# A list-ordered kernel for attention and a squared-ReLU MLP: SyncE's issues counted in the order, and other due times

## The chip, the cores and the metric

The kernel runs on one core of one Trainium2 chip. The core has five engines that each work through their own instructions in order: TensorE (PE in the profile; its weight loads are shown as PEld), VectorE (DVE), ScalarE (ACT), GpSimd (POOL) and SyncE (SP), which here issues all the DMA transfers. The metric is the time of one execution on the device in microseconds (us); less is better.

## The reference, cut to what matters

Four batches of 12480 rows of 128 numbers pass through two attention steps with 32 inducing rows, and then through an MLP with a squared ReLU:

```python
def mab(q, kv):
    s = scale * (q @ kv.transpose(0, 2, 1))
    s = s - s.max(-1, keepdims=True)
    a = np.exp(s)
    a /= a.sum(-1, keepdims=True) + 1e-09
    return a @ kv
h = mab(I, x)        # 32 x 128 for each batch: needs all 12480 rows
out = mab(x, h)      # 12480 x 128
...
r = np.maximum(out @ w_in, 0.0)      # d_ff = 2048
return (r * r) @ w_out
```

So each batch has a first softmax over all of its rows, which gives h, and only then a second softmax for each row, and the MLP.

## The kernel before, in words

**The work.** Each batch is cut into 26 chunks of 480 rows (104 chunks in all), and the chunks into 7 groups of four (the last group has two). As the second attention step is linear in h, the kernel multiplies h with the weights first and writes the squared ReLU as sums over pairs of the 32 attention weights. What is left for each chunk is, by the names of the jobs in the code:

- `ups` (L1035): four matmuls from the attention weights `dT` into `hp`, two at a time;
- `lifts` (L1051): two ScalarE squares of `hp` into `g`;
- `downs` (L1063): five matmuls into `po`, the last of which (L1075) takes `dT` with `lin`;
- `evictions` (L1082): `po` to `o`, on ScalarE or VectorE; `stores` (L1096): one DMA to the output.

Around the chunks lie, for each batch:

- `x_loads` (L588): 7 loads of x transposed into 7 buffers `xp`; `row_loads` (L597): 13 loads of half a group of x rows into 5 buffers `xnb`, the last of them made of 5 DMAs;
- `first_softmax` (L607): scores of a group against the inducing rows (8 fp32 matmul instructions, L369 with `indT_sb`), evicted by VectorE with a running maximum (L625); then the maximum over all; then `exponents` (L655, ScalarE), `transposes` (L663, VectorE, L671), and `row_sums` (L676), where TensorE multiplies the exponents with the rows (L694), which ends in h (L715);
- `readings` (L719): scores of a group against h (L369 with `hT`), which is the last use of that group's `xp` buffer; then `attention` (L745), nine steps over VectorE, GpSimd and ScalarE that end with a DMA of the weights to a scratch tensor `ad` (L781);
- `squares` (L785): three DMAs that load `dT` back (L516), and then `square` (L798): a small matmul `sq` (L805), a VectorE eviction (L813), a GpSimd square (L819), and one DMA for each chunk of the group that puts the result into the last 32 rows of `dT` (L822). The group's `downs` need it;
- `prepare` (L826), `pair_weights` (L994) and `pair_sums` (L1013): from h to the batch's weights.

The first softmax of batch 0 runs ahead of all that, in a function of its own.

**The order.** From there to the end, the order of the instructions on each engine is written out when the program is built. Each job above is a generator that yields operations. `op(engines, took, due, *needs)` names the engine, a cost in us, a due time and marks or rings of buffers that must be free. The class `Order` (L77) keeps a clock for each engine. At each step it finds the operation that could start earliest; among the operations of that engine that could start within PATIENCE of it, it takes the one with the earliest due time (L120 to L123). So a due time is a rank among those that are ready, and not a time at which anything starts. Once the program runs, an engine takes its instructions in the order found, and waits for what isn't there.

The due times hang on three things. `nominal(n)` is LEAD + PERIOD x n for chunk n; a batch's first chunk is n = 26 b. `h_due(b)`, the due time of h, is that of the chunk AHEAD chunks before the batch's first (L585). A group's X, around which attention and squares are placed, is a fixed time ahead of its first chunk, with SLACK in it (L726, L790). The numbers before are PERIOD 2.95, LEAD 33.0, SLACK 6.0, AHEAD 17.

**SyncE in the order.** An operation on SP costs SyncE 0.06 us, however many DMAs it has. `moved` is the time at which the transfers so far have been moved. No SP operation starts before `moved - QUEUED`, with QUEUED 3.0:

```python
if engines == "SP":
    return max(t, self.free["SP"], self.moved - QUEUED), "SP"
...
    self.free["SP"] = start + 0.06
    self.moved = max(self.moved, start) + took
    end = max(start + LAND, self.moved + LAND - 0.7)
```

Of the kernel before, what the change touches and what calls it, by code (L numbers as in the profile page):

```python
# [25 lines left out]
CH = 4 * TP  # L26
# [16 lines left out]
SLOTS = 8  # L43
PERIOD = 2.95
LEAD = 33.0
SLACK = 6.0
AHEAD = 17
QUEUED = 3.0
PATIENCE = 0.12
SPARE = 0.3  # L50
LAND = 3.2
LATE = {"PE": 0.25, "ACT": 0.2, "DVE": 0.15, "POOL": 0.25}
# [24 lines left out]
class Order:  # L77

    def __init__(self):
        self.free = {"PE": 0.0, "ACT": 0.0, "DVE": 0.0, "POOL": 0.0, "SP": 0.0}  # L80
        self.moved = 0.0
        self.jobs = []

# [13 lines left out]
    def when(self, job):  # L97
        engines, took, due, needs, alone = job[1]
        t = 0.0 if alone else job[2]
        for n in needs:  # L100
            r = n.ready()
            if r is None:
                return None
            t = max(t, r)
        if engines == "SP":
            return max(t, self.free["SP"], self.moved - QUEUED), "SP"
        if "|" in engines:
            act, dve = max(t, self.free["ACT"]), max(t, self.free["DVE"])
            return (act, "ACT") if act + SPARE < dve else (dve, "DVE")
        return max(t, self.free[engines]), engines  # L110

    def run(self):
        while self.jobs:
# [11 lines left out]
            if engine == "SP":  # L125
                self.free["SP"] = start + 0.06
                self.moved = max(self.moved, start) + took
                end = max(start + LAND, self.moved + LAND - 0.7)
            else:
                self.free[engine] = start + took  # L130
                end = start + took + LATE[engine]
# [4 lines left out]

def op(engines, took, due, *needs, alone=False):
    return engines, took, due, needs, alone


@with_exitstack
def attend_then_relu2_mlp(ctx: ExitStack, tc: tile.TileContext, xn, xT, indT, w_in, w_out, outT):
# [445 lines left out]
    def x_loads():  # L588

        for b in range(1, NB):  # L590
            for G, w in enumerate(WID):
                end = yield op("SP", 2.6 * w / CH, h_due(b) - 30 - 2.0 * (NG - G), xp_ring, alone=True)
                xp_ring.held.append(mark("read", b, G))
                sts[b].xp[G] = load_xT(b, G, flow, NX)
                mark("x", b, G).t = end

    def row_loads():  # L597

        for b in range(1, NB):
            for h in range(HALVES):  # L600
                i = h % XB
                end = yield op("SP", 1.4, h_due(b) - 24 + 1.3 * h, xnb_free[i], alone=True)
                sts[b].rows[h] = load_half(b, h, xnb[i])
# [3 lines left out]
    def first_softmax():  # L607

        for b in range(1, NB):
# [5 lines left out]
            for G, w in enumerate(WID):  # L615
                due = H - 23 - 1.2 * (NG - G)
                yield op("PE", 0.85, due, att, mark("x", b, G))
# [37 lines left out]
    def exponents(b, sT, nb, zs):  # L655

        for G, w in enumerate(WID):
            end = yield op("ACT", 0.69, h_due(b) - 17 + 2.0 * G, mark("nb", b), alone=True)
            s = sT[:, 480 * G:480 * G + w]
# [3 lines left out]
    def transposes(b, sT):  # L663

        sts[b].en = {}
        for G, nb32 in enumerate(BLK):
            end = yield op("DVE", 0.62, h_due(b) - 15.5 + 2.0 * G, mark("exp", b, G), en_ring, alone=True)
            mark("summed", b, G)
# [7 lines left out]
    def row_sums(b, zs):  # L676
# [5 lines left out]
        for G, nb32 in enumerate(BLK):  # L682
            for h in range(2 * G, min(2 * G + 2, HALVES)):
                needs = [mark("rows", b, h), mark("en", b, G)] + ([] if hacc else [att])
                t0 = 8 * (h - 2 * G)
                t1 = min(t0 + 8, nb32)
                end = yield op("PE", 0.075 * (t1 - t0), H - 14 + 2.0 * G, *needs)
                if hacc is None:
# [30 lines left out]
    def readings():  # L719

        for b in range(NB):
            st = sts[b]
            for G in range(NG):
                w, t = WID[G], BLK[G]
                wb = 32 * t
                X = nominal(NCH * b + 4 * G) - 14 - SLACK  # L726
                due = X - 9
                if b < NB - 1:
                    due = min(due, h_due(b + 1) - 32 - 2.0 * (NG - G))
                end = yield op("PE", 0.85, due, att, mark("h", b))  # L730
# [14 lines left out]
    def attention(b, G, e, X, since, gone):  # L745
# [33 lines left out]
        nc.vector.scalar_tensor_tensor(a16[:, 1, 0:w], a[:, 0:w], lessen, a16[:, 0, 0:w], op0=ALU.add, op1=ALU.subtract)  # L779
        end = yield op("SP", 0.7, X)  # L780
        nc.sync.dma_start(st.ad[:, :, :, 480 * G:480 * G + w].rearrange("q i h n -> (q i) h n"), a16[:, :, 0:w])  # L781
# [3 lines left out]
    def squares():  # L785

        for b in range(NB):
            st = sts[b]
            for G, n in enumerate(GRP):
                X = nominal(NCH * b + 4 * G) - 11 - SLACK  # L790
                rows = slice(0, MI * n)
                end = yield op("SP", 1.1, X, mark("ad", b, G), dT_ring, alone=True)
                dT_ring.held.append(mark("over", b, G))
# [4 lines left out]
    def square(b, G, n, X, rows, dT):  # L798

        st = sts[b]  # L800
        yield op("PE", 0.1 * n, X + 4, mark("dT", b, G), mark("single", b), po_ring)
        done = po_ring.take()
        ps = ps_o.tile([P, 512], F32, tag="po", name=f"sq_{b}_{G}")
        for j in range(n):
# [3 lines left out]
            )  # L808
        end = yield op("DVE", 0.72, X + 4.2, z_ring)
        done.t = end  # L810
        done = z_ring.take()
        z = mlp.tile([P, CH], F32, tag="z", name=f"z_{b}_{G}", bufs=2)
        nc.vector.tensor_scalar(z[rows], ps[rows, 0:CH], st.off[rows], cut[rows], op0=ALU.add, op1=ALU.max)  # L813
        end = yield op("POOL", 1.05, X + 5.5, zz_ring)
        done.t = end
# [3 lines left out]
        nc.gpsimd.tensor_tensor(g[rows], zv[rows], zv[rows], op=ALU.mult)  # L819
        end = yield op("SP", 0.12 * n, X + 7)  # L820
        for j in range(n):
# [274 lines left out]
    def stores():  # L1096

        for n, (b, c) in enumerate(CHUNKS):
            end = yield op("SP", 0.65, nominal(n + 1.5), mark("out", n), alone=True)
            nc.sync.dma_start(outT[:, b, c], outs.pop(n))  # L1100
            mark("stored", n).t = end
# [216 lines left out]
```

## Time and profile before

| what | value |
|---|---|
| runs | 429.43, 425.01, 428.63 us; median 428.63 |
| the profiled execution | 426.38 us |
| its span, from the first to the last instruction | 424.6 us |
| mean granted TensorE clock | 0.958 |
| instructions | 8741 |
| moved by DMA | 94.29 MB, 222 GB/s |

How to read the profile: it is one execution, with times in us unless marked ns. A row of a group names the line, the engine, the operation, what is written and read (`out<-in`), the shapes and the count; then come the busy time, the mean duration in ns, the idle time of the engine just before these instructions, and what ended most of it. In a row of one line of the source, the three durations are least, median and greatest in ns. In a table of stretches each row is a stretch in us from the start of the span, with each engine's busy time in it, the granted TensorE clock as a share of full speed (PEclk), and the share of the DMA engines. SPq is SyncE's queue of DMA issues; a row `A <- B` of a table of waits says that A waited for B, in us in total, times, and longest.

### The profile page before, as it was taken

The page shows a single profiled execution, that of the slowest core. Times are in us where ns is not written, and L with a number is a line of the kernel's source. Part 1 is how long each engine was busy: PE and PEld are TensorE (multiplying, and loading weights), DVE is VectorE, ACT ScalarE, POOL GpSimd, SP SyncE. Part 2 cuts the span into 40 slices and gives each one's busy share as a digit, 9 for nine tenths or more (in the row PEclk, how much of TensorE's full clock was granted, in tenths as well). Part 3 has the DMA queues.
Part 4 walks back from the last instruction along what each step waited for, and adds up shares of the span by engine and source line. Part 5 has one row for each costly group of instructions (what it writes and reads, how often), then busy time and mean ns, then how long its engine had stood idle before and what let it go on. Part 6 is the DMA issues. An engine that isn't in the chain of part 4 may idle for free.

```text
span 424.6 us, 8741 instructions
## 1 busy us (share of the span) xinstructions
PE 357.0 (84%) x3077; PEld 169.2 (40%) x3077; DVE 329.9 (78%) x879; ACT 285.4 (67%) x394; POOL 83.3 (20%) x93
## 2 busy tenths in 40 slices
PE   0993736999789799989889899998799999998894
PEld 0662504533334245423434254324344455333341
DVE  7859889899566499989844789989646999997541
ACT  1464231477967498666966795769676987886894
POOL 1000011151210122242300312142110302343010
PEclk9997985799899899999999999999899999999999
DMA  7972566645596998856797978954985243456742
GB/s 273 416 248 64 188 248 223 209 150 170 144 334 211 329 345 259 294 173 214 209 354 234 322 271 264 325 182 152 293 289 168 95 154 106 159 153 212 209 142 96
DMA packets 63760, 94.29 MB, mean 222 GB/s; under 512 B 22880, under 2 KB 53856, under 8 KB 63712
## 3 DMA queue, kind: packets, MB, share of 16 engines
q1 hardware_dynamic: 63712, 93.69, 66.9%
q8 instruction: 25, 0.41, 0.4%
q14 instruction: 23, 0.19, 0.1%
HBM read 58.52 MB, written 31.95 MB: 213 GB/s over the span
## 4 chain that ended last, share of the span: by engine, by line
PE 46%; DVE 25%; DMA 16%; ACT 6%; issue 4%; SPq 2%; DVEq 0%; ACTq 0%
PE po L1074 12%; PE hp L1045 11%; DMA xnb<-xn_dram 7%; PE s L369 7%; DMA dT<-ad 4%; DMA ad<-a 4%; PE hacc L694 4%; DVE G L1008 3%; ACT g L1059 3%; PE po L1075 3%; PE xt L391 2%; DVE scored L741 2%; DMA outT_dram<-o 1%; DVE o L1093 1%; PE sq L805 1%
## 5 line engine op out<-in xcount | busy, mean ns | idle before, releaser
L1059 ACT ACTIVATE g<-hp 128x960 f16<-128x960 f32 x208 | 193.7, 969 | 63.7 <-PE hp L1045 62.5
L1045 PE MATMUL hp<-dT,pairs 96*128 96x480 f16 x416 | 111.3, 371 | 6.2 <-ACT g L1059 6.0
L1074 PE MATMUL po<-g,w 128*128 128x480 f16 x416 | 104.0, 372 | 0.9 <-DVE o L1093 0.8
L1093 DVE TENSOR_SCALAR o<-po,osc,bias 128x480 f32<-128x480 f32 x60 | 46.1, 768 | 44.8 <-PE po L1075 34.2
L1045 PEld LDWEIGHTS <-pairs 96*128 96x128 f16 x416 | 35.2, 99 | 62.9 <-issue 39.1
L1074 PEld LDWEIGHTS <-w 128*128 128x128 f16 x416 | 39.1, 99 | 49.8 <-issue 12.2
L757 POOL TENSOR_TENSOR scored<-scored,mx 128x480 f32<-128x480 f32 (+1 forms) x28 | 26.6, 953 | 144.5 <-DVE k L289 71.0
L819 POOL TENSOR_TENSOR zz<-z 128x480 f16<-128x480 f32 (+1 forms) x28 | 28.8, 1028 | 90.7 <-DVE z L813 76.8
L766 POOL TENSOR_TENSOR scored<-scored,z 128x480 f32<-128x480 f32 (+1 forms) x28 | 26.9, 959 | 87.0 <-DVE z L764 62.0
L1091 ACT ACTIVATE o<-po,bias,osc 128x480 f32<-128x480 f32 x44 | 33.1, 755 | 11.2 <-PE po L1075 4.1
L1075 PE MATMUL po<-dT,lin 128*128 128x480 f16 x104 | 38.8, 373 | 0.0
L694 PE MATMUL hacc<-xnb,en 128*32 128x128 f32 x588 | 24.3, 283 | 9.1 <-DMA xnb<-xn_dram 4.7
L369 PE MATMUL s<-xp,hT 128*32 128x480 f32 (+1 forms) x224 | 28.3, 579 | 2.4 <-DVE scored L741 2.3
L813 DVE TENSOR_SCALAR z<-sq,off,cut 128x480 f32<-128x480 f32 (+1 forms) x28 | 21.5, 768 | 9.1 <-PE sq L805 8.9
L369 PE MATMUL s<-xp,indT_sb 128*32 128x480 f32 (+1 forms) x224 | 27.1, 555 | 1.6 <-DVE sT L408 0.9
L694 PEld LDWEIGHTS hacc<-xnb,en 128*32 128x32 f32 x588 | 15.8, 111 | 21.9 <-DVE en L671 7.4
L1008 DVE TENSOR_TENSOR G<-hwp,hw 128x512 f16<-128x512 f16 x64 | 23.8, 431 | 0.6 <-PE wq L1024 0.5
L394 ACT COPY xp<-xt 128x896 f32<-128x896 f32 (+1 forms) x13 | 12.3, 956 | 17.8 <-PE xt L391 17.8
L759 ACT ACTIVATE scored<-scored 128x480 f32<-128x480 f32 (+1 forms) x28 | 16.0, 575 | 9.6 <-POOL scored L757 9.3
L779 DVE SCALAR_TENSOR_TENSOR a<-a,lessen,a 128x480 f16<-128x480 f32 (+1 forms) x28 | 20.5, 733 | 1.0
L671 DVE STREAM_TRANSPOSE en<-sT 128x480 f32<-128x480 f32 (+1 forms) x21 | 13.0, 632 | 9.2 <-PE hacc L694 9.0
L1024 PE MATMUL wq<-w_hi,G 128*128 128x128 f16 x256 | 16.9, 219 | 2.1 <-ACT w L1028 1.0
(228 smaller groups left out, 443.4 us busy)
## 6 DMA issues: line engine op xcount, KB each, us to landing
outT_dram<-o SPq DMA_DIRECT2D x104, 240.0 KB, 2.7
xp<-xT_dram SPq DMA_DIRECT2D x18, 960.0 KB, 6.2
xnb<-xn_dram SPq DMA_DIRECT2D x21, 512.0 KB, 6.8
xnb<-xn_dram SPq DMA_DIRECT2D x23, 448.0 KB, 5.9
dT<-ad SPq DMA_DIRECT2D x72, 120.0 KB, 2.7
ad<-a SPq DMA_DIRECT2D x24, 240.0 KB, 2.6
dT<-zz SPq DMA_DIRECT2D x104, 30.0 KB, 2.0
wi<-w_in_dram SPq DMA_DIRECT2D x4, 512.0 KB, 5.6
```

The lines of the kernel that those rows point to most:

```text
L369: nc.tensor.matmul(ps[32 * q:32 * q + 32, 0:w], lhsT, xp[:, w * q:w * q + w], start=True, stop=True,)
L694: nc.tensor.matmul(hacc[32 * q:32 * q + 32, 0:P], st.en[G][:, t], xg[:, t % 8], start=G == 0 and t < 4, stop=G == NG - 1 and t + 4 >= nb32,)
L757: nc.gpsimd.tensor_tensor(e[:, 0:t], e[:, 0:t], mx[:, 0:t].unsqueeze(2).broadcast_to([P, t, MI]), op=ALU.subtract)
L766: nc.gpsimd.tensor_tensor(e[:, 0:t], e[:, 0:t], z[:, 0:t].unsqueeze(2).broadcast_to([P, t, MI]), op=ALU.mult)
L819: nc.gpsimd.tensor_tensor(g[rows], zv[rows], zv[rows], op=ALU.mult)
L1008: nc.vector.tensor_tensor(g[:, :, MI * j:MI * j + n], hwp[:, :, 0:n], hw16f[:, :, s0:s0 + n], op=ALU.mult)
L1045: nc.tensor.matmul(hp[:, i, 0:CH].rearrange("p (q t) -> p q t", q=4), pairs[0:96, (2 * j + i) * P:(2 * j + i + 1) * P], dT[0:96], start=Tr ...
L1059: nc.scalar.activation(gs[n][:, 2 * j:2 * j + 2], hps.pop((n, j))[:, 0:2, 0:CH], AF.Square)
L1074: nc.tensor.matmul(po[:, 0:CH], st.w16[:, i], g[:, i], start=i == 0, stop=False)
L1075: nc.tensor.matmul(po[:, 0:CH].rearrange("p (q t) -> p q t", q=4), st.lin, dT, start=False, stop=True)
L1091: nc.scalar.activation(o, po[:, 0:CH], AF.Identity, bias=st.bias, scale=st.osc)
L1093: nc.vector.tensor_scalar(o, po[:, 0:CH], st.osc, st.bias, op0=ALU.mult, op1=ALU.add)
```

## The change

No instruction is added or removed. What changes is the numbers and the account by which the order is found:

- SyncE's operations are named with their DMAs (`"SP3"` for three). Each costs 0.273 us (ISSUE), and none is issued before the eighth last one has landed (LANES). The limit on what is queued (QUEUED, now 0.792) holds for the bulk loads of x and rows alone, which have `hold` set; these also can't start before their due time less 46.229 (HOLD). A landing is LAND (now 2.676) after the transfer is moved.
- Due times: PERIOD, LEAD, SLACK, AHEAD get other values, and so do the offsets of x loads, row loads, first scores, exponents, transposes, row sums, readings and small squares.
- Other costs for the loads and stores.

```diff
-PERIOD = 2.95
-LEAD = 33.0
-SLACK = 6.0
-AHEAD = 17
-QUEUED = 3.0
-PATIENCE = 0.12
-SPARE = 0.3
-LAND = 3.2
+PERIOD = 2.053
+LEAD = 6.003
+SLACK = 6.456
+AHEAD = 35.782
+QUEUED = 0.792
+PATIENCE = 0.129
+SPARE = 0.066
+LAND = 2.676
+LANES = 8
+X_AT = 45.453
+ROWS_AT = 38.336
+ROWS_STEP = 5.125
+S1_AT = 2.09
+EXP_AT = 13.468
+EXP_STEP = 1.721
+SUM_AT = 38.792
+READ_AT = 16.42
+READ_STEP = 0.085
+READ_UNTIL = 65.662
+SQ_AT = 11.979
+ISSUE = 0.273
+HOLD = 46.229
...
+        if hold is not None:
+            t = max(t, due - hold)
...
-        if engines == "SP":
-            return max(t, self.free["SP"], self.moved - QUEUED), "SP"
+        if engines.startswith("SP"):
+            t = max(t, self.free["SP"], self.landed[-LANES])
+            return (t if hold is None else max(t, self.moved - QUEUED)), "SP"
...
-                self.free["SP"] = start + 0.06
-                self.moved = max(self.moved, start) + took
-                end = max(start + LAND, self.moved + LAND - 0.7)
+                n = int(job[1][0][2:] or 1)
+                t = start
+                for _ in range(n):
+                    t = max(t, self.landed[-LANES]) + ISSUE
+                    self.moved = max(self.moved, t) + took / n
+                    self.landed.append(max(self.moved, t + 0.3) + LAND)
+                self.free["SP"] = t
+                end = self.landed[-1]
...
-                end = yield op("SP", 2.6 * w / CH, h_due(b) - 30 - 2.0 * (NG - G), xp_ring, alone=True)
+                end = yield op("SP", 3.0 * w / CH, h_due(b) - X_AT - 2.0 * (NG - G), xp_ring, alone=True, hold=HOLD)
...
-                end = yield op("SP", 1.4, h_due(b) - 24 + 1.3 * h, xnb_free[i], alone=True)
+                end = yield op("SP" if h < HALVES - 1 else "SP5", 1.5, h_due(b) - ROWS_AT + ROWS_STEP * h, xnb_free[i], alone=True, hold=HOLD)
...
-                due = H - 23 - 1.2 * (NG - G)
+                due = H - S1_AT - 1.2 * (NG - G)
...
-            end = yield op("ACT", 0.69, h_due(b) - 17 + 2.0 * G, mark("nb", b), alone=True)
+            end = yield op("ACT", 0.69, h_due(b) - EXP_AT + EXP_STEP * G, mark("nb", b), alone=True)
...
-            end = yield op("DVE", 0.62, h_due(b) - 15.5 + 2.0 * G, mark("exp", b, G), en_ring, alone=True)
+            end = yield op("DVE", 0.62, h_due(b) - EXP_AT + 1.5 + EXP_STEP * G, mark("exp", b, G), en_ring, alone=True)
...
-                end = yield op("PE", 0.075 * (t1 - t0), H - 14 + 2.0 * G, *needs)
+                end = yield op("PE", 0.075 * (t1 - t0), H - SUM_AT + EXP_STEP * G, *needs)
...
-                due = X - 9
+                due = X - READ_AT
                 if b < NB - 1:
-                    due = min(due, h_due(b + 1) - 32 - 2.0 * (NG - G))
+                    due = min(due, h_due(b + 1) - READ_UNTIL - READ_STEP * (NG - G))
...
-                end = yield op("SP", 1.1, X, mark("ad", b, G), dT_ring, alone=True)
+                end = yield op("SP3", 1.4, X, mark("ad", b, G), dT_ring, alone=True)
...
-        yield op("PE", 0.1 * n, X + 4, mark("dT", b, G), mark("single", b), po_ring)
+        yield op("PE", 0.1 * n, X + SQ_AT, mark("dT", b, G), mark("single", b), po_ring)
...
-        end = yield op("SP", 0.12 * n, X + 7)
+        end = yield op(f"SP{n}", 0.16 * n, X + SQ_AT + 3)
...
-            end = yield op("SP", 0.65, nominal(n + 1.5), mark("out", n), alone=True)
+            end = yield op("SP", 0.69, nominal(n + 1.5), mark("out", n), alone=True)
```

The eviction and the GpSimd square of a small square move with SQ_AT too (0.2 and 1.5 us after it), and the DMA to `ad` has a cost of 0.95 in place of 0.7.

More of the change, by code (lines that the diff above doesn't have):

```diff
@@ L81, in __init__ @@
         self.moved = 0.0
+        self.landed = [0.0] * LANES
         self.jobs = []
@@ L97, in when @@
     def when(self, job):
-        engines, took, due, needs, alone = job[1]
+        engines, took, due, needs, alone, hold = job[1]
         t = 0.0 if alone else job[2]
+        if hold is not None:
+            t = max(t, due - hold)
         for n in needs:
@@ L134, in run, with op @@
             self.step(job, end)
-def op(engines, took, due, *needs, alone=False):
-    return engines, took, due, needs, alone
+def op(engines, took, due, *needs, alone=False, hold=None):
+    return engines, took, due, needs, alone, hold
 @with_exitstack
@@ L779, in attention @@
         nc.vector.scalar_tensor_tensor(a16[:, 1, 0:w], a[:, 0:w], lessen, a16[:, 0, 0:w], op0=ALU.add, op1=ALU.subtract)
-        end = yield op("SP", 0.7, X)
+        end = yield op("SP", 0.95, X)
         nc.sync.dma_start(st.ad[:, :, :, 480 * G:480 * G + w].rearrange("q i h n -> (q i) h n"), a16[:, :, 0:w])
@@ L808, in square @@
             )
-        end = yield op("DVE", 0.72, X + 4.2, z_ring)
+        end = yield op("DVE", 0.72, X + SQ_AT + 0.2, z_ring)
         done.t = end
@@ L813, in square @@
         nc.vector.tensor_scalar(z[rows], ps[rows, 0:CH], st.off[rows], cut[rows], op0=ALU.add, op1=ALU.max)
-        end = yield op("POOL", 1.05, X + 5.5, zz_ring)
+        end = yield op("POOL", 1.05, X + SQ_AT + 1.5, zz_ring)
         done.t = end
```

## The prediction

> **What bounds the kernel now.** I read the page first, then the stretches between the landmarks of the trace, then TensorE's groups with their idle time, and last SyncE and its transfers. From the page, the span, the engines, and the busy tenths in 40 slices:
>
> ```profile
> span 424.6 us, 8741 instructions
> PE 357.0 (84%) x3077; PEld 169.2 (40%) x3077; DVE 329.9 (78%) x879; ACT 285.4 (67%) x394; POOL 83.3 (20%) x93
> ...
> PE   0993736999789799989889899998799999998894
> ...
> DVE  7859889899566499989844789989646999997541
> ...
> PEclk9997985799899899999999999999899999999999
> ```
>
> TensorE is the busiest engine, but the share is a mean over different stages. The first output product tells where the stage that the change governs begins to deliver:
>
> ```profile
> L1075 PE MATMUL po<-dT,lin x104: 364/366/607, 88.8 to 418.3; 128*128 128x480 f16 x104
> L369 PE MATMUL hw<-w_in_sb,hT x32: 592/604/617, 53.5 to 323.4; 128*32 128x512 f32 x32
> L715 DVE TENSOR_TENSOR hT<-hs,zr x3: 191/191/191, 137.8 to 322.2; 128x32 f32<-128x32 f32 x3
> ```
>
> The 104 chunks end between 88.8 and 418.3 us, one every 3.20 us (329.5 / 103). The list order rules from about 53.5 us, when batch 0's h is there. So there are three stages: the start up to 53.5 (not touched), the filling from 53.5 to 88.8, and the loop from 88.8 on. The busy times in these stretches, and in the last 51.6 us:
>
> ```profile
> core 0: us, PE busy (x) PEld busy (x) DVE busy (x) ACT busy (x) POOL busy (x), PEclk, DMA share, GB/s
> 53.50:88.80 35.30, 24.60 (x251) 13.43 (x252) 31.01 (x99) 12.44 (x20) 7.06 (x7) 0.76 0.65 225
> 88.80:181.80 93.00, 85.33 (x744) 37.67 (x742) 72.14 (x195) 69.46 (x100) 21.80 (x24) 0.96 0.77 253
> 181.80:273.90 92.10, 83.10 (x745) 37.09 (x744) 72.33 (x191) 67.27 (x95) 19.45 (x20) 1.00 0.80 258
> 273.90:373.00 99.10, 91.80 (x777) 41.20 (x775) 81.77 (x211) 77.18 (x107) 24.69 (x25) 0.98 0.56 182
> 373.00:424.60 51.60, 41.05 (x209) 17.77 (x206) 29.22 (x57) 37.98 (x44) 9.15 (x10) 0.99 0.51 163
> ```
>
> In the filling VectorE is the bound (31.0 of 35.3 us busy), TensorE has 10.7 us free. In the loop TensorE is (301.3 of 335.8 us), with VectorE and ScalarE well below. What the loop can give back is TensorE's idle time. By its groups in the loop (busy us, mean ns, then idle before and what ended it):
>
> ```profile
> L1045 PE MATMUL hp<-dT,pairs 96*128 96x480 f16 x404 | 107.8, 370 | 6.2 <-ACT g L1059 6.0
> ...
> L694 PE MATMUL hacc<-xnb,en 128*32 128x128 f32 x588 | 24.3, 283 | 9.1 <-DMA xnb<-xn_dram 4.7 <-DVE en L671 3.8 <-DVE z L762 0.6
> L369 PE MATMUL s<-xp,hT 128*32 128x480 f32 (+1 forms) x168 | 20.0, 549 | 1.3 <-DVE scored L741 1.2
> L369 PE MATMUL s<-xp,indT_sb 128*32 128x480 f32 (+1 forms) x160 | 19.1, 548 | 0.1
> ...
> L805 PE MATMUL sq<-dT,singles 96*32 96x480 f16 x100 | 10.7, 379 | 6.7 <-DMA dT<-ad 6.4 <-ACT o L1091 0.2
> ...
> L851 PE MATMUL bank<-ssq,every 128*128 128x1 f32 x6 | 1.3, 278 | 2.8 <-ACT hws L842 2.8
> ```
>
> The row sums (L694) cost 9.1 us of waiting, half of it for rows, the small squares (L805) 6.7 us, nearly all for their load; the ups (L1045) 6.2. Those three are 22.0 of some 28 us (335.8 - 301.3, less 6.3 after the last output product).
>
> **The change part by part.** The chip's instructions and bytes stay the same; only the order on the in-order engines moves. So each term is a wait that goes or comes, or work that moves between a stage with room and one without.
>
> SyncE's account. Old: 0.06 us for an operation; new: 0.273 for each DMA of it, and an order that looks at the eighth last landing. The trace has, in ns and then us to landing:
>
> ```profile
> L822 SPq DMA_DIRECT2D dT<-zz x104: 585/599/1357, 80.2 to 407.6; - x104
> L516 SPq DMA_DIRECT2D dT<-ad x84: 303/424/1614, 69.9 to 400.2; - x84
> L1100 SPq DMA_DIRECT2D outT_dram<-o x104: 332/376/1521, 90.7 to 419.5; - x104
> ...
> xnb<-xn_dram SPq DMA_DIRECT2D x21, 512.0 KB, 6.8
> ...
> dT<-ad SPq DMA_DIRECT2D x72, 120.0 KB, 2.7
> ```
>
> A square's four pieces hold SyncE 4 x 0.599 = 2.4 us where the old account had 0.06 and the new has 1.1. A group's three loads take 3 x 0.424 = 1.3 us plus 2.7 to land, about 4.0. The old account gave max(3.2, 1.1 + 2.5) = 3.6 us, the new 0.273 + 1.4 + 2.676 = 4.35. Old was short by 0.4 us, new is not. I cost the account itself at nothing and let it act through the waits below; a queue still counted at half for the squares is a rival's ground.
>
> Small squares. Before, due X + 4 and the load due X: 4 us apart by due times, about the landing time itself. After, X + 11.979, with X in the new units, 12 us apart. The wait of 6.7 us should nearly vanish; bounds: all 6.7 gone, or none. Above that, an eviction, a GpSimd square and four pieces still follow; by due times the squares come (17.456 - 11.979) / 2.053 = 2.7 chunks ahead of the group's first, 8.5 us at 3.20 us a chunk; if that cover is short, outputs wait. I take 4.7 off: the load counted right, 2 us left for bursts.
>
> Row sums. Half-loads: old account 1.4 + 2.5 = 3.9 us plus up to 3.0 of allowed backlog; new 0.273 + 1.5 + 2.676 = 4.45 plus up to 0.79. The 6.8 measured comes with the backlog of 3.0; taking 2.2 of it away leaves 4.6, near the account. The exponents' dues go from 2.0 to 1.72 us apart, but in the new units that is 0.84 chunk a group against 0.68, and their place is 19 chunks earlier, so en too has time. Bounds: 9.1 us gained, or each late group paid (a rival). I take 6.0 off, two thirds.
>
> The first softmax's place. h's due goes from 17 chunks ahead of its batch to 35.8; the scores from 27.6-25.2 chunks ahead of it to 40.9-37.4. For batch 1 that falls into the filling. What comes with it: the scores' evictions and the reading of their accumulator, and later the transposes:
>
> ```profile
> L671 DVE STREAM_TRANSPOSE en<-sT 128x480 f32<-128x480 f32 (+1 forms) x21 | 13.0, 632 | 9.2 <-PE hacc L694 9.0
> L625 DVE TENSOR_SCALAR_CACHE_REDUCE sT<-s 128x480 f32<-128x480 f32 (+1 forms) x21 | 12.7, 604 | 1.5 <-PE s L369 1.0
> ...
> L625 DVE DVE_READ_ACCUMULATOR sT<-s 128x1 f32 x21 | 1.7, 81 | 0.0
> ```
>
> One group of seven already lies there. Six more cost VectorE 6 x (0.604 + 0.081) = 4.1 us, and the maximum's chain about 1: the first output comes some 5 us later, as VectorE had only 4.3 us free there, scattered in waits. In return the loop loses six of its twenty groups of scores (x160, eight instructions each), 6/20 of TensorE's 19.1 us: 5.7 us. Net -0.6. Bounds: +5 if the loop's TensorE time is not what counts, -8.7 if batch 1's row sums (24.3 / 3 = 8.1 us) also fit into TensorE's free time. The seven readings of batch 0 move ahead of its preparation as well, but the loop's x168 are the 21 of the other batches, so these lay before 88.8 already. Batches 2 and 3: part of their first softmax leaves the stretches of the row sums, where VectorE has its slack (the runs 5664, 44 and 646 of its tenths), for one nearer the previous preparation; 11 us of VectorE work a batch (7 x 0.68 + 7 x 0.63 + 2). In the loop VectorE has over 20 us free a batch, so I cost it at nothing; without that cover it would be up to 22 us for two batches.
>
> On the clock: between 60 and 80 us it is low.
>
> ```profile
> 60.00:70.00 10.00, 4.65 (x76) 2.83 (x76) 9.49 (x32) 1.30 (x3) 2.32 (x2) 0.57 0.65 245
> 70.00:80.00 10.00, 7.97 (x49) 4.43 (x49) 8.46 (x33) 0.97 (x1) 1.92 (x2) 0.57 0.71 234
> ```
>
> The Trainium skill ("TensorE: Matmul & The Clock Gate", Part 1: The HAM clock gate) says that the gate opens only after sustained activity, some 3.4 us. By that rule, scores put into these 20 us would hold the clock up and shorten 12.6 us of matmuls by up to 5.4; the trace agrees that the clock is low there, at 0.57. The sum doesn't take it, since VectorE is at 18.0 of these 20 us (9.49 + 8.46).
>
> The sum, against the profiled execution (426.38 us, of which 424.6 span): -4.7 - 6.0 - 0.6 = -11.3, so 415.1. That execution lies 2.25 us under the median of the three runs (428.63) and inside their 425.01 to 429.43; the mean of all four is 427.4, and 427.4 - 11.3 gives **416 us**.
>
> **The rivals.**
>
> *The stalls only move* (427, from 424 to 431). Due times rank what is ready and start nothing. The new hold at 46.229 never binds: the last x load is due at 45.2, so released at -1.0, and the last rows, due at 115.8, at 69.6, long before their buffers are free. An x load needs a free buffer, so a reading:
>
> ```profile
> SPq L364 <- PE s L369: 26.7, 10, 10.0
> ```
>
> SyncE stood 26.7 us for that (10.0 of it at a time), and with it all that was queued behind. With issues counted at 0.273 against 0.376 to 0.599, the queue drifts again and the waits come back elsewhere. For: that row. Against: the load waits named above have a direct answer in the account.
>
> *Rows land late* (slower, 441). The row sums now have almost the highest rank on TensorE, 50 to 55 chunks ahead of their batch by due, so TensorE turns to them as soon as the account says that rows are there: after 4.45 us. If landing stays at 6.8, everything behind in TensorE's queue, ups and downs too, waits 2.35 us. Of 13 halves of a batch 5 load ahead into free buffers, leaving 4 groups, 12 in three batches: 12 x 2.35 = 28, less the 9.1 paid now, less 4.7 from the squares: +14 to +15. It decides from a median landing of about 5.5 us on; against: less backlog is allowed. The Trainium skill ("DMA: Bandwidth & Descriptors", Rules for kernel authors) speaks for this rival: issue a transfer early and wait for it late, while the change holds bulk loads back until 0.79 us of backlog is left; no run here shows yet which counts for more.
>
> *All of it works* (403). Squares 6.7, row sums 9.1 and 8.7 net at the filling: 427.4 - 24.5. For: TensorE's 10.7 free us in the filling. Against: VectorE is full there, and rows must land.
>
> **How the numbers follow.** The forecast has 0.47 (its own range 406 to 423), the moved stalls 0.21, late rows 0.15, all of it 0.17. The range 402 to 431 takes in the forecast, the moved stalls and most of the best case, leaving out the late rows and the rest of the best: about 2 in 10. About 1% is what this kernel's runs can tell from no change. Faster by over 1%: 0.47 + 0.17 + 0.04 of the moved stalls, 0.68; within 1%: 0.14; slower: 0.15 + 0.03, 0.18.
>
> **What would show it.** Right: the idle before L805 at 2 us or less, before L694 at 3 or less; six more score groups of batch 1 before the first output product, which comes at 92 to 95 us; the first of the three L715 at 100 to 115 instead of 137.8; row loads landing in 4.5 to 5 us; from first to last output product about 312 us instead of 329.5. The forecast is wrong if the first product comes after 98, if L694's idle grows, if outputs wait for late square pieces, or if ScalarE's lifts or VectorE end more of TensorE's waits than the 6.2 now at L1045.

## The result, and the profile after

The changed kernel takes 409.4 us (median of four runs, 406.34 to 413.17) against 427.63 us for the kernel before (four runs): a ratio of 0.954, with a 95% interval of 0.945 to 0.963. The ratio goes by the fast runs: the 413.17 us, over 1.5% above the fastest, is left out of it, so it differs a little from the quotient of the medians. The forecast was 416 us with a range of 402 to 431. The profiled execution of the changed kernel took 411.6 us, of which 409.8 are its span; before it was 426.38 and 424.6. A line number after is the one before plus 23.

From the page of the kernel after, the span, the two engines and the granted clock in 40 slices:

```profile
span 409.8 us, 8708 instructions
PE 352.2 (86%) x3077; PEld 169.2 (41%) x3077; DVE 330.6 (81%) x879; ACT 284.1 (69%) x394; POOL 84.1 (21%) x93
...
PE   0893766787999899898999999979899999998993
...
DVE  8859879778969799996979899986377999996541
...
PEclk9998898689999999998999999999999999999998
```

The same work is done: the counts of matmuls (3077), of VectorE's, ScalarE's and GpSimd's instructions and of DMAs are those of before. The 33 fewer instructions of the page (8708 against 8741) are semaphore waits. TensorE's busy time is 352.2 us where it was 357.0. The 14.8 us lie between the stages. The last matmul of each output chunk, and the h of batches 1 to 3:

```profile
L1098 PE MATMUL po<-dT,lin x104: 364/366/607, 100.1 to 403.3; 128*128 128x480 f16 x104
L738 DVE TENSOR_TENSOR hT<-hs,zr x3: 191/191/191, 122.8 to 301.1; 128x32 f32<-128x32 f32 x3
```

The first output product comes 11.3 us later (88.8 before), but from first to last it takes 303.2 us where it took 329.5, so 26.3 us less; what follows is 6.5 us, as against 6.3. Each h stands about 15 to 21 us earlier. The busy time in the filling and the loop, from the stretches of the kernel after:

```profile
53.50:100.10 46.60, 35.13 (x386) 17.33 (x386) 38.59 (x120) 16.71 (x35) 9.26 (x8) 0.85 0.66 220
100.10:409.80 309.70, 285.81 (x2334) 129.69 (x2332) 248.59 (x630) 246.20 (x329) 73.63 (x76) 0.99 0.75 235
```

From the first product to the end TensorE has 285.8 us of work where it had 301.3 (-15.5), and 23.9 us idle where it had 34.5 (-10.6). The sum of both is 26.1. Its groups in that stretch, with the idle time before them; the prediction shows the groups of before, but for the downs (L1074 there), which had 413 matmuls, 103.4 us and a mean of 373 ns, with 0.9 us idle before them:

```profile
L1068 PE MATMUL hp<-dT,pairs 96*128 96x480 f16 x400 | 107.0, 368 | 0.7 <-ACT g L1082 0.6
L1097 PE MATMUL po<-g,w 128*128 128x480 f16 x413 | 102.0, 369 | 2.9 <-DVE o L1116 2.7
...
L717 PE MATMUL hacc<-xnb,en 128*32 128x128 f32 x512 | 21.3, 278 | 8.7 <-DMA xnb<-xn_dram 6.7 <-DVE z L787 1.9
L392 PE MATMUL s<-xp,hT 128*32 128x480 f32 (+1 forms) x168 | 20.0, 549 | 0.3 <-DVE scored L764 0.3
L392 PE MATMUL s<-xp,indT_sb 128*32 128x480 f32 (+1 forms) x112 | 13.3, 548 | 0.5 <-DMA xp<-xT_dram 0.3 <-issue 0.2
...
L828 PE MATMUL sq<-dT,singles 96*32 96x480 f16 x96 | 10.2, 375 | 0.8 <-DVE o L1116 0.8
```

Six groups of first scores have left the loop (160 to 112 instructions, -5.8 us), and with them 76 row sums (-3.0 us). The squares no longer wait for their load. The row sums wait as before, now more for their rows. The ups' wait for ScalarE is gone.

The loop's gain does not lie where batch 1's scores left it. From each batch's first output product to the next batch's (the last row to the end of the span), in us, with TensorE's busy time, the groups of first scores and the matmuls of row sums that lie there:

| stretch | us before, after | TensorE busy | score groups | row sums |
|---|---|---|---|---|
| filling | 35.3, 46.6 | 24.6, 35.1 | 1, 7 | 0, 76 |
| batch 0 | 93.0, 91.2 | 85.3, 83.9 | 7, 7 | 196, 226 |
| batch 1 | 92.1, 83.4 | 83.1, 81.0 | 7, 7 | 196, 180 |
| batch 2 | 85.9, 75.5 | 79.5, 69.9 | 6, 0 | 196, 106 |
| batch 3 | 64.8, 59.6 | 53.4, 51.1 | 0, 0 | 0, 0 |

Each batch's first scores have moved ahead: batch 1's fill the filling, batch 2's take their place in the stretch of batch 0, batch 3's that of batch 1. It is the stretch of batch 2 that has no first scores left. The landing times, in KB and median us:

```profile
outT_dram<-o SPq DMA_DIRECT2D x104, 240.0 KB, 3.5
...
xnb<-xn_dram SPq DMA_DIRECT2D x21, 512.0 KB, 5.5
...
dT<-ad SPq DMA_DIRECT2D x72, 120.0 KB, 3.8
...
dT<-zz SPq DMA_DIRECT2D x104, 30.0 KB, 3.0
```

Rows land sooner (6.8 before), but the loads for the squares later (2.7 before). The squares' wait went although their load slowed. By due times the load now lies 12 us ahead of the square, not 4; the run with the old distance, below, shows that this is a part of it (the wait is 3.9 us there, 0.8 with the new distance and 6.7 before).

### The profile page after: what moved, and what is told of

Its sections match the earlier page's. It is cut to its first block, busy times and chain, and to the rows that moved or that the text cites. A ratio compares the mean times of both kernels' runs of the same rounds, so it can differ in the third digit from the quotient of the medians.

```text
span 409.8 us, 8708 instructions
## 1 busy us (share of the span) xinstructions
PE 352.2 (86%) x3077; PEld 169.2 (41%) x3077; DVE 330.6 (81%) x879; ACT 284.1 (69%) x394; POOL 84.1 (21%) x93
## 4 chain that ended last, share of the span: by engine, by line
PE 45%; DVE 28%; DMA 13%; ACT 4%; issue 4%; SPq 4%; POOL 0%; DVEq 0%; ACTq 0%; POOLq 0%
PE po L1097 12%; PE hp L1068 11%; PE s L392 7%; DMA xnb<-xn_dram 5%; DVE o L1116 3%; PE hacc L717 3%; PE po L1098 3%; ACT g L1082 3%; DMA ad<-a 2%; DVE G L1031 2%; PE xt L414 2%; DMA xp<-xT_dram 2%; DMA outT_dram<-o 2%; SPq L845 2%; DVE z L785 2%
## 5 line engine op out<-in xcount | busy, mean ns | idle before, releaser
L1097 PE MATMUL po<-g,w 128*128 128x480 f16 x416 | 102.6, 369 | 2.9 <-DVE o L1116 2.7
L842 POOL TENSOR_TENSOR zz<-z 128x480 f16<-128x480 f32 (+1 forms) x28 | 29.8, 1066 | 114.1 <-DVE z L836 71.0
L1114 ACT ACTIVATE o<-po,bias,osc 128x480 f32<-128x480 f32 x44 | 33.1, 751 | 11.3 <-PE po L1098 8.5
L392 PE MATMUL s<-xp,indT_sb 128*32 128x480 f32 (+1 forms) x224 | 30.1, 608 | 6.0 <-DVE sT L648 3.1
L392 PE MATMUL s<-xp,hT 128*32 128x480 f32 (+1 forms) x224 | 26.7, 549 | 4.8 <-DVE scored L764 3.1
L1031 DVE TENSOR_TENSOR G<-hwp,hw 128x512 f16<-128x512 f16 x64 | 27.0, 481 | 0.0
L764 DVE STREAM_TRANSPOSE scored<-s 128x480 f32<-128x480 f32 (+1 forms) x28 | 17.9, 640 | 4.2 <-PE s L392 4.0
L785 DVE TENSOR_REDUCE z<-scored 128x15 f32<-128x480 f32 (+1 forms) x28 | 16.8, 598 | 3.7 <-ACT scored L782 3.7
L799 DVE TENSOR_SCALAR_CACHE_REDUCE a<-a,lessen 128x480 f16<-128x480 f32 (+1 forms) x28 | 18.5, 660 | 0.5 <-DMA ad<-a 0.5
```

Of the source, the lines that this page charges most:

```text
L392: nc.tensor.matmul(ps[32 * q:32 * q + 32, 0:w], lhsT, xp[:, w * q:w * q + w], start=True, stop=True,)
L1031: nc.vector.tensor_tensor(g[:, :, MI * j:MI * j + n], hwp[:, :, 0:n], hw16f[:, :, s0:s0 + n], op=ALU.mult)
L1097: nc.tensor.matmul(po[:, 0:CH], st.w16[:, i], g[:, i], start=i == 0, stop=False)
L1114: nc.scalar.activation(o, po[:, 0:CH], AF.Identity, bias=st.bias, scale=st.osc)
```

## The experiments

The change has two halves: the account of SyncE, and the due times. The theory at the start was that the due times earn the gain and the account serves them. The first five kernels take the halves apart, then single parts. All ratios are to the kernel before, timed on the same chip in the same session, with 95% intervals.

**The new account alone.** The kernel after with all due times of before; PATIENCE, and SPARE, which weighs ScalarE against VectorE for an eviction, stay as after.

```diff
-PERIOD = 2.053
+PERIOD = 2.95
...
-SUM_AT = 38.792
+SUM_AT = 14.0
...
-HOLD = 46.229
+HOLD = 1000000.0
```

> The new account of SyncE (0.273 us for each DMA, eight lanes, backlog limit 0.792 for bulk loads alone, new landing time) with all due times as before; the hold is put out of reach. Theory A (the due times make the gain: batch 1's first softmax moves into the filling and squares move away from their loads): within 1% of before, 423 to 431 us, first output product near 89 us, TensorE waiting some 5 us at the small squares. Rival B (the account makes the gain, since SyncE's queue is then ordered as it runs): 408 to 416 us, with SyncE's waits well below those of before.

Measured: 440.2 us, 1.030 [1.025, 1.035]. Both theories missed it: with the old due times the new account costs 3%. Products stop at each border between batches, for 14.4, 23.5 and 27.4 us; the last two h come at 240.3 and 342.4 us, against 229.9 and 322.2 before. Stretches of this kernel ahead of the last border and in it (columns as in the prediction):

```profile
300.00:310.00 10.00, 6.68 (x59) 3.00 (x51) 4.94 (x11) 6.39 (x10) 1.99 (x2) 0.83 0.64 145
...
340.00:352.50 12.50, 11.72 (x73) 4.33 (x72) 10.08 (x28) 9.64 (x14) 2.00 (x2) 1.00 0.21 81
352.50:379.90 27.40, 18.17 (x191) 12.13 (x189) 24.83 (x76) 9.31 (x16) 5.22 (x5) 0.69 0.23 68
```

In the stop VectorE is at 24.8 of 27.4 us, with the preparation of the last batch's weights, which can't start before its h. ScalarE, which serves the chunks, has 9.3. In the 30 us before, the row loads stand in SyncE's queue one by one between outputs, square loads and square pieces.

**The new due times alone.** The old account, costs and limits (PATIENCE and SPARE too), the new due times.

```diff
-QUEUED = 0.792
+QUEUED = 3.0
...
-            t = max(t, self.free["SP"], self.landed[-LANES])
-            return (t if hold is None else max(t, self.moved - QUEUED)), "SP"
+            return max(t, self.free["SP"], self.moved - QUEUED), "SP"
...
+                self.free["SP"] = start + 0.06
+                self.moved = max(self.moved, start) + took
```

> All due times as changed, with the account of SyncE, the costs of loads and stores, and the limits PATIENCE and SPARE as before. Theory A: 408 to 418 us, first output product at 97 to 101 us and a loop some 20 us shorter than before's 329.5. Rival B: 423 us or more, since the order then again misjudges the queue.

Measured: 425.8 us, 0.991 [0.986, 0.996], as rival B. Theory A's gain is not there: the due times alone give 1%. The timeline of SyncE in this kernel (start, us held, queue, line, count; its line numbers are six lower than those of the kernel after) shows a part of why:

```profile
54.07 11.74 SPq L381 DMA_DIRECT2D xp<-xT_dram  x7
...
123.30 13.60 SPq L381 DMA_DIRECT2D xp<-xT_dram  x7
...
138.30 4.27 SPq L839 DMA_DIRECT2D dT<-zz  x4
...
199.62 12.12 SPq L381 DMA_DIRECT2D xp<-xT_dram  x6
```

x loads are written in runs of seven and six. Each needs the buffer of a reading, so the run holds SyncE for 12 to 14 us, and the square pieces behind it start at 138.3. Products stop from 125.7 to 151.3 us, and again from 212.1 to 221.9, right behind the third run. The runs do not explain all: ahead of the downs that end the first stop, TensorE waits for VectorE's evictions of batch 2's first scores, up to 149.5, and a third stop, from 261.8 to 272.0, has no such run ahead of it. In the kernel after, the same loads of batch 2 go singly, with square pieces between them:

```profile
120.57 2.64 SPq L845 DMA_DIRECT2D dT<-zz  x4
124.41 0.41 SPq L387 DMA_DIRECT2D xp<-xT_dram  x1
126.85 5.45 SPq L845 DMA_DIRECT2D dT<-zz  x4
132.40 0.54 SPq L387 DMA_DIRECT2D xp<-xT_dram  x1
135.86 0.50 SPq L387 DMA_DIRECT2D xp<-xT_dram  x1
```

**The limit on bulk loads, with the new due times.** `QUEUED = 0.792` becomes `QUEUED = 3.0` in the kernel after.

> The changed kernel with the backlog limit for bulk loads at 3.0, as before, in place of 0.792; the issues stay counted. Theory C (what the account adds is the low backlog limit on bulk loads alone, which lets small transfers in between; without it seven x loads in a row hold SyncE while it waits for readings, as in the run with the due times alone): 417 to 426 us, a stretch of 8 us or more of x loads alone in SyncE's queue, and chunks that wait for their square's pieces. Rival D (the counted issues do it): 407 to 412 us.

Measured: 415.1 us, 0.967 [0.962, 0.972], between the two theories' ranges. The stretch of x loads that theory C asks for is not there: in the loop they go singly or in pairs here too (1.8 us for the longest pair), and SyncE waits 18.6 us on the readings. So the runs of seven are undone without the tight limit, by the rest of the account.

**The limit, with the old due times.** The same edit in the kernel with the new account alone.

> The run with the account alone (old due times), with the backlog limit for bulk loads at 3.0 as before. Theory C (there the low limit made the row loads yield to every small transfer, so that h and the weights came late and the chunks stood still at the batches' borders): the last h comes at 320 to 330 us instead of 342, the three stops at the borders shrink below 8 us each, and the time falls to 418 to 429 us. Rival (with issues counted the chunks outrun h at the old due times whatever the limit): 436 to 442 us and the same stops.

Measured: 424.0 us, 0.990 [0.984, 0.995], as theory C had it: the last h comes at 318.3, and the border stops are 9.1, 2.5 and 1.4 us. So the tight limit made the loss of the first experiment. The four together with the kernels before and after:

| | old account | new account, limit 3.0 | new account, limit 0.792 |
|---|---|---|---|
| old due times | 1 | 0.990 | 1.030 |
| new due times | 0.991 | 0.967 | 0.954 and 0.962 |

Neither half does it alone. Late bulk loads hurt where the first softmax has 17 chunks of lead; where it lies a batch ahead they do no harm that can be told.

**The price of an issue.** `ISSUE = 0.273` becomes `ISSUE = 0.06` in the kernel after.

> The changed kernel with 0.06 us in place of 0.273 for a DMA's issue; eight lanes, the limits, landing time and due times stay. Theory C: 406 to 413 us, no difference beyond the spread of the runs. Rival D (issues must be counted for the order to hold): 417 us or more, with more SyncE time behind waits for GpSimd's squares and readings.

Measured: 413.5 us, 0.965 [0.960, 0.969]. That is just above theory C's range, far from rival D's, and can't be told from the kernel after: with the price cut to a fifth the time rises by some 1% at most. So the account's price of an issue, the part that gives the change its name, is not what matters most. What is left is the rule of the eighth last landing, the landing time and the transfers' prices, and PATIENCE and SPARE, which went back together with them in the run with the due times alone; these were not tried one by one.

**Small squares as before.** `SQ_AT = 11.979` becomes `SQ_AT = 4.0`.

> The changed kernel with the small squares due 4 us after their load, as before, in place of 11.979 (their eviction, GpSimd square and copies move with them). Theory A: TensorE's wait at the small squares returns from 0.8 to some 5 us and the time rises to 413 to 416 us. Rival: 407 to 411 us, because the loads' own due times now lie 8.5 chunks ahead and the wait is gone whatever the squares' place.

Measured: 413.8 us, 0.964 [0.957, 0.971]. This is theory A's wait and time, near the lower ends. The squares wait 3.9 us again, and the ups 5.9 (0.7 after), while the row sums wait 4.3 where it was 8.7. So of these 8 us of waits half is paid back in the same run, and in the time they hardly show: 0.964 is at most one percent over the kernel after.

**The first softmax of batch 1 out of the filling.** Its scores are due 30 later, all else as after.

```diff
-                due = H - S1_AT - 1.2 * (NG - G)
+                due = H - S1_AT - 1.2 * (NG - G) + (30.0 if b == 1 else 0.0)
```

> The changed kernel with batch 1's first scores due 30 us later, so that they rank behind the first chunks and leave the filling to batch 0. Theory E (work put into the filling is only shifted: it delays the first output product as much as it shortens the loop): first product at 88 to 93 us instead of 100.1, a loop longer by 6 to 11 us, 405 to 413 us in all. Rival F (the filling's free TensorE time is where the gain comes from): 416 us or more. Rival G (the delay of the first product was a cost that can be had back): 398 to 404 us.

Measured: 431.0 us, 0.998 [0.993, 1.003]: the whole gain is lost, the time of rival F. The first product comes at 93.3, 5 to 7 us sooner than in the two profiles of the kernel after (98.3 and 100.1); but h of batch 1 comes at 151.5, and products then stop once, from 158.7 to 190.0 us. So the 5 us that the prediction put on these scores in the filling are about right; what they buy is far more than the 5.7 us of TensorE work.

**A filling without the late start, two ways.** First, batch 0's preparation due 40 sooner:

```diff
-        F = nominal(NCH * b)
+        F = nominal(NCH * b) - (40.0 if b == 0 else 0.0)
```

> The changed kernel with the due times of batch 0's preparation 40 us earlier, so that in the filling it ranks ahead of batch 1's first scores. Theory A with the filling's delay as a separate price: first output product at 91 to 95 us instead of 100.1, the loop's 303 us kept, 402 to 406 us in all. Rival (VectorE and TensorE work is only shifted; what isn't done in the filling comes back in the loop): 407 to 411 us with a loop longer by as much as the first product is earlier.

Measured: 415.1 us, 0.971 [0.967, 0.976], slower than both said, with h of batch 1 at 130.4 instead of 122.8. The weights were there at 92.7 us, but the first product came at 99.2: the first square pieces were issued from 94.9 on, and TensorE's last wait ahead of the downs, until 98.1, was for batch 1's maximum. So, second, the first group's reading, attention and squares 40 sooner as well:

```diff
-                X = nominal(NCH * b + 4 * G) - 14 - SLACK
+                X = nominal(NCH * b + 4 * G) - 14 - SLACK - (40.0 if b + G == 0 else 0.0)
...
-                X = nominal(NCH * b + 4 * G) - 11 - SLACK
+                X = nominal(NCH * b + 4 * G) - 11 - SLACK - (40.0 if b + G == 0 else 0.0)
```

> The changed kernel with batch 0's preparation and the attention and square of its first group due 40 us earlier, so that all that the first output product needs ranks ahead of batch 1's first scores, which still fill the gaps. Theory E (work is only shifted): first product at 91 to 94 us instead of 100.1, loop 309 to 312 us instead of 303, 407 to 412 us in all. Rival G (the late first product was a cost to be had back): the loop stays below 305 and the time is 399 to 405 us. Rival H (batch 1's first softmax is what must not be late: an h later by some us moves the whole chain of batches): 414 us or more, with the first of the three h after 128 us and stops of over 8 us in the loop.

Measured: 421.2 us, 0.985 [0.980, 0.990], as rival H. The first product comes at 92.2, h of batch 1 at 135.4, and products stop from 146.0 to 162.7. What the filling saves at the front comes back behind, with more.

**Row loads counted as landing later.** The measured landing of 5.5 us, a good 1 us over the account's 4.45, goes into the account.

```diff
-                mark("rows", b, h).t = end
+                mark("rows", b, h).t = end + 1.0
```

> The changed kernel with rows held to land 1.0 us later in the order's account alone (4.45 to 5.45 us, the measured median being 5.5), so that row sums are placed later on TensorE. If the 8.7 us before the row sums are what the short account costs, they fall to 4 us or less and the time by 2 to 5 us, to 404 to 408. Rival: the time stays within 407 to 412 us, since a later place for the row sums makes h later, or the waits come from the burst itself and not from the account.

Measured: 416.4 us, 0.970 [0.965, 0.974]. The group of the row sums from the first product on, in this kernel, and the stretch of a stop that it has and the kernel after has not:

```profile
L717 PE MATMUL hacc<-xnb,en 128*32 128x128 f32 x512 | 20.7, 278 | 2.9 <-DMA xnb<-xn_dram 2.1 <-DVE en L694 0.8
```

```profile
237.50:260.80 23.30, 18.24 (x215) 9.66 (x214) 21.02 (x70) 7.33 (x12) 3.66 (x4) 0.93 0.73 248
```

The wait fell from 8.7 to 2.9 us, as meant, and the time did not. Other waits came in its place: the squares wait 4.3 us (0.8 after), nearly all for their load, and the ups 2.7 (0.7 after). In the stop VectorE is at 21.0 of 23.3 us. Its timeline (start, us, engine, line) shows what held the products:

```profile
235.30 0.38 PE L828 MATMUL sq<-dT,singles 96*32 96x480 f16 x2
...
237.49 0.37 PE L1098 MATMUL po<-dT,lin 128*128 128x480 f16 x1
...
259.23 0.76 DVE L836 TENSOR_SCALAR z<-sq,off,cut 64x480 f32<-64x480 f32 x1
259.89 0.56 PEld L1097 LDWEIGHTS <-w 128*128 128x128 f16 x4
259.94 0.97 PE L1097 MATMUL po<-g,w 128*128 128x480 f16 x4
```

A small square stands finished in one of the two buffers `po` (the last kernel's expectation calls them PSUM buffers) from 235.7 on. Its eviction ranks on VectorE behind the next batch's preparation and first scores, and comes at 259.2. One more product fits into the other buffer; the next downs need this one, and start as it is free. The stops of two kernels above look the same: with the first group sooner, square at 143.6, eviction at 160.7, downs at 161.8; with batch 1's scores later, square at 156.4, eviction at 185.2, downs at 188.5.

**The kernel after once more**, on the chip of the last two runs.

> The changed kernel once more, unchanged, beside the next two on the same chip, for the spread: 407 to 413 us, a ratio to before of 0.95 to 0.965. If it is 0.96 or more, the runs with the squares' old place and with issues at 0.06 can't be told from it; if 0.955 or less, both parts are worth something.

Measured: 412.2 us, 0.962 [0.956, 0.968], with the first product at 98.3 and the last at 399.5 us. So on the same chip the two runs above took 421.2 and 416.4 us against 412.2.

**The eviction of the squares first.** The last kernel moves that eviction ahead of the pile.

```diff
-        end = yield op("DVE", 0.72, X + SQ_AT + 0.2, z_ring)
+        end = yield op("DVE", 0.72, X + SQ_AT + 0.2 - 60, z_ring)
```

> The kernel with row loads counted 1 us later, and besides each small square's eviction on VectorE (line 836 of the kernel after) due 60 us earlier, so that it goes as soon as its matmul is done. In the run without this edit, output products stopped from 237.5 to 260.8 us, while a square stood finished in one of the two PSUM buffers it shares with the output products (matmul 235.3, eviction 259.2). Theory P (the shared buffer is what the stop costs): no square waits over 4 us for its eviction, that stop of 23.3 us is gone, the row sums still wait 3 to 4 us in the loop, and the time falls from 416 to 400 to 409. Rival V (the stop only shows that VectorE has a pile to do for the next batch, and the time is needed anyway): the stop of 23 us goes too, but shorter stops or a later border between batches come in its place, and the time stays at 412 to 419.

Measured: 415.1 us, 0.966 [0.956, 0.975]. Rival V: no square waits over 3 us for its eviction, the stop of 23.3 us is gone, and the time is that of the kernel without the edit, 0.970, within what can be told. The row sums wait 4.5 us and the ups 5.2, so the waits have moved again. In place of the one stop there are two others, from 115.8 to 133.1 and from 347.0 to 355.9 us. In this kernel the shared buffer chose where the products stopped; it did not make the time. The edit was not tried on the other two kernels. The first of these stops is longer than the 7.8 us that the kernel after has at the same chunk, and its stretches show a second thing, the granted clock (the third number from the end):

```profile
114.00:116.00 2.00, 1.83 (x10) 0.68 (x7) 1.97 (x3) 1.37 (x2) 0.59 (x1) 1.00 1.05 347
116.00:117.00 1.00, 0.21 (x4) 0.02 (x3) 0.98 (x3) 0.00 (x0) 0.00 (x0) 1.00 1.07 334
117.00:118.00 1.00, 0.62 (x14) 0.35 (x14) 0.98 (x2) 0.55 (x1) 0.00 (x0) 1.00 0.82 225
118.00:119.00 1.00, 0.23 (x4) 0.14 (x4) 0.07 (x1) 0.20 (x1) 0.61 (x1) 0.81 0.75 185
119.00:120.00 1.00, 1.00 (x6) 0.28 (x3) 0.59 (x1) 0.00 (x0) 0.00 (x0) 0.50 0.75 260
...
131.00:132.00 1.00, 1.00 (x8) 0.00 (x0) 0.96 (x4) 0.00 (x0) 0.00 (x0) 0.50 1.00 351
132.00:133.00 1.00, 1.00 (x8) 0.39 (x5) 0.83 (x2) 0.00 (x0) 0.00 (x0) 0.86 1.32 299
```

After 3 us with TensorE at a third, 13 us run at half clock, though TensorE is busy in nearly all of them. That is one execution, of 415.7 us; others of this kernel took 408.6 to 416.7. No version beat the kernel after.

## Why the prediction was right, and where it was wrong

**Small squares: right.** Forecast -4.7 us with at most 2 left; the wait is 0.8, so -5.9. With the old place it is 3.9.

**Row sums: wrong.** Forecast -6.0 us with at most 3 left; the wait is 8.7, so -0.4. The step "taking 2.2 of it away leaves 4.6, near the account" failed: 512 KB of rows land in 5.5 us. The landing is not the whole of it: with the landing counted later the wait is 2.9, but it is also 3.6 with the cheaper issue and 4.3 with the squares' old place. In none of these orders did the smaller wait bring time.

**The first softmax into the filling: right in kind, far off in size.** Forecast +5 in the filling and -5.7 of TensorE's work in the loop, net -0.6. Measured +11.3 in the filling and -15.5 of TensorE's busy time in the loop, net -4.2. (The other 10.6 us of the loop are waits.) The six groups of scores are 5.8 us, as forecast. The prediction itself said that it would be wrong if the first product came after 98, and it came at 100.1 (98.3 in the second run); the first of the three h was forecast for 100 to 115 us and came at 122.8. Of the 11.3 us, 5 to 7 are batch 1's scores; the rest is not theirs, as the product came at 93.3 without them, and what it is stays open. On the other side, the working priced only the scores that change their stage, and missed more: 3.0 us in row sums, 2.7 in ups, downs and products, whose means are 2 to 5 ns shorter (the granted clock of the loop is 0.99 where it was 0.98), and the rest in small groups and overlap. The clock in the filling rose: 60 to 80 us had 0.57 before, and now (columns as above):

```profile
60.00:70.00 10.00, 4.99 (x44) 0.86 (x40) 9.64 (x32) 1.68 (x3) 1.00 (x1) 0.91 0.91 364
70.00:80.00 10.00, 8.20 (x103) 3.77 (x96) 7.86 (x27) 0.45 (x2) 0.99 (x1) 0.67 1.02 313
```

The prediction left out of its sum the rule of the Trainium skill ("TensorE: Matmul & The Clock Gate", Part 1: The HAM clock gate) that the gate opens only after sustained activity. The trace agrees as to the clock, 0.91 and 0.67, though TensorE's busy time in these 20 us rose only from 12.6 to 13.2; that the added scores raised it is not shown.

Above all, the prediction did not price what an early h of batch 1 lets the later batches do. Batch 1's first product came 44 us after its h before (181.8 - 137.8) and 68.5 us after (191.3 - 122.8), and in that room the next batch's first softmax moves ahead (the table of stretches above). In the kernels that change only what is due in the filling, the time follows this h:

| kernel | h of batch 1 | ratio |
|---|---|---|
| after, two sessions | 122.8, 121.0 | 0.954, 0.962 |
| preparation sooner | 130.4 | 0.971 |
| preparation and first group sooner | 135.4 | 0.985 |
| batch 1's scores later | 151.5 | 0.998 |

That the due time of batch 1's scores decides, with the new account, is shown; which of the waits it spares is not, since the waits move with every order.

**SyncE's account costed at nothing: wrong.** It is worth 2.4 to 3.7% with the new due times (0.991 to 0.967, and to 0.954 or 0.962), and -3% with the old ones at the tight limit. The step that let it act "through the waits below" missed the queue itself: a load that waits for a buffer holds all behind it, 13.6 us for one run of seven. The row that the prediction quoted for its first rival, SyncE waiting 26.7 us on the readings, points there: it is 36.4 us with the due times alone, and 19.6 in the kernel after. Which part of the account undoes the runs is open; neither the limit nor the price of an issue does it alone.

**The ups: not forecast.** -5.5 us. The wait came back with the squares' old place (5.9), but also with their new one in the last kernel (5.2), so what removes it is open.

**The rivals.** That stalls only move (427) did not happen to the change, but it did to three of its variants (the first group sooner, the rows' landing, the eviction first): each mended one wait and paid at another place. Rows that land late (441): they do land at 5.5 us, the point from which that rival decides, but TensorE pays 8.7 us for them and not 28; why so little is open. The Trainium skill's advice ("DMA: Bandwidth & Descriptors", Rules for kernel authors) to issue early and wait late is borne out with the old due times, where holding bulk loads back costs 4% (0.990 to 1.030), and not with the new ones. Of all of it works (403) the squares came true, and of batch 1's row sums 76 of 196 fit into the filling; the wait of the row sums stayed.

The sum was forecast at -11.3. In the profiled executions it is: squares -5.9, row sums' wait -0.4, ups -5.5, TensorE's other waits +1.2, its busy time in the loop -15.5, the filling +11.3; in all -14.8. That the forecast of the time came near is luck in good part, as errors cancelled: the row sums gave 5.6 us less than their term and the filling took 6.3 us more, while the ups and the moved work gave some 15 us that no term had.

## What to carry to other kernels

Price a change of order at the stage that releases the next one (here h), not only at the waits in view: without the 5 to 7 us that batch 1's scores take in the filling, the whole gain of 4% was gone. When a list order is changed, look at every in-order queue for runs of transfers that wait for the same kind of buffer; a run of seven held everything behind it for 13.6 us. And a wait that is mended counts only when the time falls: here a wait of 6 us and a stop of 23 us went away, others came in their place, and the time stayed.

## What the runs showed of the hardware

- The spread of one kernel goes with the granted clock. The kernel after has spans of 404.5 us at a mean clock of 0.985, 405.4 at 0.974, 404.6 at 0.973, 409.8 at 0.966 and 411.4 at 0.960, some 3 us for each 0.01. The kernel before has a mean clock of 0.956 over 54 executions (two far outliers, of 519.6 and 868.5 us, left out), the kernel after of 0.970 over 11. By these 3 us, an estimate, about 4 us of the gain go with the clock. Whether the clock makes the span, or pauses of TensorE make both, was not separated.
- A pause need not be complete: in one execution TensorE was at 0.21, 0.62 and 0.23 of three successive us, the clock fell from 1.00 to 0.50 in the third, and it came back after 13 us in which TensorE was busy for 12.6.
- The small transfers got slower in the faster kernel: outputs land in 3.5 us where it was 2.7, and 30 KB pieces in 3.0 where it was 2.0. From the first product to the end the core moved 235 GB/s instead of 220; whether that is the cause was not tried.
